# Low words of the weights and the pooled sums of a batch's q and k on VectorE instead of GpSimd

## The chip, the cores and the metric

One core of one Trainium2 chip runs the kernel. The metric is the time of one execution in microseconds, as the device measures it; less is better. The engines are named as in the profile: PE (TensorE, its matmuls), PEld (its weight loads), DVE (VectorE), ACT (ScalarE), POOL (GpSimd) and SP (SyncE), whose queue issues the DMAs. Each engine works through its own queue in order.

## What is computed

A batch of 8, 8 heads, 576 positions, 64 values per head; 512 is the width of the model and 2048 that of the hidden layer.

```python
q_d, k_d, v_d = (t.reshape(B, H, S // 4, 4, D).mean(axis=3) for t in (q, k, v))
out_up = np.repeat(softmax_attention(q_d, k_d, v_d), 4, axis=2)      # pooled attention
out_local = attention within |i - j| < 4                             # local attention
x = (out_up + out_local) as [B, S, H * D]
xn = (x - mean(x)) / sqrt(var(x) + 1e-6) * g_ln
out = x + maximum(xn @ w_ch1, 0) @ w_ch2
```

The weights w_ch1 and w_ch2 come as float64.

## The kernel before

Every part of the work is a task of a planner (class Plan): an engine, a duration that the planner assumes, a function that issues the instructions, the tasks it depends on, a due time, and buffers that it takes and gives back. `order()` puts all tasks into one list by these assumed times, task by task the one that can start first and, among those within 0.5 us, the one due first. The instructions are issued in that order, so it is also the order of each engine's queue. The planner's costs are simple lines (for VectorE 0.06 + n / 950 us for n elements per partition, for GpSimd 0.13 + 0.0022 n); they know of no effect of one engine on another. For a load it assumes 2.5 us to land (`LAT`) behind its issue, and counts its bytes at 260 GB/s. A task with `alt` may go to a second engine, whichever suits the planner's clock.

**The weights.** Sixteen blocks f of the hidden layer have a piece of w_ch1 and of w_ch2 each, 32 pieces of 128x512 float64 numbers. Each is split into a high and a low word of TensorE's 32-bit format fp32r. `weights` makes the tasks: SP loads the raw words (lines 347 and 352); ACT takes the upper half (line 359, two instructions); DVE shifts it (line 367) and puts in bits of the lower half (line 370, two instructions on 128x256); ACT makes the high word by a cast (line 378); the low word is a subtraction (line 383), which the planner gives to DVE, or to POOL where that is free sooner (with 0.3 us added). In the profile the intermediate is cva, the words are hi and lo.

**Pooled attention.** For the first batch the sums of four positions of q and k are made from the transposed windows of local attention. For every other batch and half of the heads, `pooled_half` loads q, k and v in two halves each into one of two staging buffers (raw2q is q of the second batch's first half of heads, raw3q of its second half; line 700) and adds up four positions by two instructions: 72x512 in place (line 713) and 72x256 (line 714). These are on POOL; the condition `by_dve` at line 716 holds for no task that there is, since the first batch loads v alone here. The staging buffer is given back when both are through. Transposes on PE (line 739), copies on ACT (lines 748 and 752), scores, their maximum (lines 770 and 771, DVE), exponentials and the product with v follow.

**The hidden layer.** 18 chunks c of 256 rows go through 8 pairs p of blocks. `up` (line 996) multiplies three combinations of words into PSUM, `relu` (line 1003, ACT) makes the high word hh, `rest` (line 1007, DVE) the low word hl, `down` (line 1019) adds three combinations into the accumulators. The weights are made once and stay in SBUF, so only the first chunks, between about 56 and 190 us, run while the weights are being prepared; local and pooled attention of the second batch are prepared in the same time.

Of the kernel before, what the change touches and what calls it, by code (L numbers as in the profile page):

```python
# [9 lines left out]
F32 = mybir.dt.float32  # L10
# [12 lines left out]
class Plan:  # L23
# [14 lines left out]
    def add(self, eng, dur, fn, deps=(), due=0.0, take=(), give=(), lag=None, ahead=1e9, alt=None, kb=0):  # L38

        opts = {eng: (dur, fn, 0.0)}  # L40
        if alt is not None:
            opts[alt[0]] = alt[1:]
        t = SimpleNamespace(
            n=len(self.tasks), opts=opts, dur=dur, deps=[d for d in deps if d is not None],
            due=due, take=take, give=give, lag=lag, ahead=ahead, open=0.0, waits=0, eng=None, fn=None, kb=kb,
        )
        self.tasks.append(t)
        return t
# [91 lines left out]
def attention_then_ffn(  # L140
# [10 lines left out]
    nc = tc.nc  # L151
# [37 lines left out]
    def unit(shape, name, dtype=F32, kind="u"):  # L189
        kind = kind if kind in SEP else "u"  # L190
        return work.tile(shape, dtype, tag=kind, bufs=SEP.get(kind, NU), name=name)
# [107 lines left out]
    def pooled_at(b, pr):  # L299
        if b == 0:  # L300
            return norm_at(0) - B0G - B0G_GAP * (3 - pr)
        return g_base + b * CHUNK * S / T - (NPAIR - 1 - pr) * (CHUNK * S / T / NPAIR if b > 1 else G1)
# [16 lines left out]
    U, A, STG = (("u", 1),), (("a", 1),), (("stg", 1),)  # L319
    DMA, LAT, W_AHEAD, W_LAG = 0.5, 2.5, 40, 1.5  # L320

    def act(n, sbuf=False):
        return (0.155 if sbuf else 0.14) + n / 1430.0

    def dve(n):
        return 0.06 + n / 950.0

    def pool(n):
        return 0.13 + 0.0022 * n
# [7 lines left out]
    def weights(which, f):  # L337
        key = (which, f)
        name = f"{which}_{f}"
        due = W0 + W_GAP * (f // 2) + 0.5 * (which - 1) + 1.0 * (f % 2)  # L340

        def load():
            x = box[key] = SimpleNamespace()
            x.raw = [unit([P, 512], f"s{name}_{i}", I32) for i in range(2)]
            for i in range(2):
                if which == 1:
                    nc.sync.dma_start(
                        x.raw[i].rearrange("p (c e) -> p c e", c=KC // 2),
                        w1[256 * i : 256 * (i + 1), f * 2 * P : (f + 1) * 2 * P].rearrange("(c p) e -> p c e", p=P),
                    )  # L350
                else:
                    nc.sync.dma_start(x.raw[i], w2[f * P : (f + 1) * P, 512 * i : 512 * (i + 1)])

        def high_word():

            x = box[key]
            x.a = unit([P, 512], f"cva{name}", I32)
            for i in range(2):
                nc.scalar.activation(
                    x.a[:, 256 * i : 256 * (i + 1)].bitcast(F32),  # L360
                    x.raw[i].rearrange("p (n two) -> p n two", two=2)[:, :, 1].bitcast(F32),
                    AF.Prelu, scale=REBIAS, alpha=-(2.0**32),
                )

        def low_word():
            x = box[key]
            nc.vector.tensor_single_scalar(out=x.a, in_=x.a, scalar=3, op=ALU.logical_shift_left)
            for i in range(2):
                a = x.a[:, 256 * i : 256 * (i + 1)]
                nc.vector.scalar_tensor_tensor(  # L370
                    out=a, in0=x.raw[i].rearrange("p (n two) -> p n two", two=2)[:, :, 0], scalar=29, in1=a,
                    op0=ALU.logical_shift_right, op1=ALU.bitwise_or,
                )

        def high():
            x = box[key]
            x.hi = unit([P, 512], f"hi{name}", F32R)
            nc.scalar.copy(x.hi, x.a.bitcast(F32))

        def low(eng):  # L380
            x = box[key]
            lo = unit([P, 512], f"lo{name}", F32R)
            eng.tensor_sub(lo, x.a.bitcast(F32), x.hi.bitcast(F32))
            weight[key] = (x.hi, lo)

        add = plan.add
        t = add("SP", 1.3, load, (), due, take=(("u", 3),), lag=LAT + W_LAG, kb=512, ahead=W_AHEAD)
        t = add("ACT", 2 * act(256, True), high_word, (t,), due)
        t = add("DVE", 0.45 + 2 * dve(256), low_word, (t,), due, give=(("u", 2),))
        t = add("ACT", act(512, True), high, (t,), due, take=U)  # L390
        return add("DVE", dve(512), lambda: low(nc.vector), (t,), due, take=U, give=U,
                   alt=("POOL", pool(512), lambda: low(nc.gpsimd), 0.3))

# [280 lines left out]
    def pooled(b):  # L676
        due0 = pooled_at(b, 0)
        add = plan.add
        for hg in range(2):
            pooled_half(b, hg)  # L680

    def pooled_half(b, hg):
        add = plan.add
        i = 2 * b + hg
        x = SimpleNamespace(m={})
        vd = vds[hg]
        ready = {}
        own = b < NPB
        if own:
            ready["q"], ready["k"] = gsum_done[b, "q"], gsum_done[b, "k"]  # L690
        for nm, src in (("v", v),) if own else (("q", q), ("k", k), ("v", v)):
            for half in range(2):
                key = (nm, half)
                due = pooled_at(b, 2 * hg) - (8.0 if nm == "v" else 14.0)

                def load(src=src, key=key):
                    half = key[1]
                    raw = work.tile([P, 1024], F32, tag="stg", bufs=NSTG, name=f"raw{i}{key[0]}{half}")
                    raw = raw[:GH].rearrange("p (h e) -> p h e", h=4)
                    nc.sync.dma_start(  # L700
                        raw,
                        src[b, 4 * hg : 4 * hg + 4, half * S // 2 : (half + 1) * S // 2, :]
                        .rearrange("h (g r) d -> g h (r d)", r=FACTOR),
                    )
                    x.m[key] = raw

                def pool4(key=key, eng=nc.gpsimd):
                    nm, half = key
                    raw = x.m[key]
                    if half == 0 and nm != "v":  # L710
                        setattr(x, nm, unit([GH, 2, 4, D], f"{nm}d{i}"))
                    dst = vd if nm == "v" else getattr(x, nm)
                    eng.tensor_add(raw[:, :, : 2 * D], raw[:, :, : 2 * D], raw[:, :, 2 * D :])
                    eng.tensor_add(dst[:, half, :, :D], raw[:, :, :D], raw[:, :, D : 2 * D])

                by_dve = b == 0 and nm == "k"
                t = add("SP", 0.45, load, (), due - 4.0, take=STG, lag=LAT, kb=288, ahead=AHEAD)
                t = add(
                    "DVE" if by_dve else "POOL", dve(512) + dve(256) if by_dve else 2.1,
                    (lambda key=key: pool4(key, nc.vector)) if by_dve else pool4, [t, lastg.vd[hg] if nm == "v" else None] + ready.get(nm, []),  # L720
                    due, take=U if half == 0 and nm != "v" else (), give=STG,
                )
                ready.setdefault(nm, []).append(t)
        for pr in range(2):
            pooled_pair(b, hg, pr, x, ready)
# [345 lines left out]
    for f in range(DFF // P):  # L1071
        for which in (1, 2):
            wdone[which, f] = weights(which, f)
# [42 lines left out]
```

## Time and profile before

| | us |
|---|---|
| median of 3 runs | 1068.34 (1067.77 to 1068.43) |
| the profiled execution | 1069.49 |
| its span, first to last instruction | 1067.7 |

| engine | busy us | share of the span |
|---|---|---|
| PE | 1043.4 | 98% |
| DVE | 509.0 | 48% |
| ACT | 317.7 | 30% |
| POOL | 266.5 | 25% |

TensorE's mean granted clock is 0.990 of full speed. The profile is of one execution on the chip. Busy times are those of the engines' instructions; register, branch, semaphore and DMA-issuing instructions are not counted. Instructions of one engine overlap a little at their ends, so that two in a row take less than twice one.

### The profile page before, as it was taken

Reading aid. Unit: us, or ns where it says so; the run is one execution under the profiler, and the core shown is the slowest. Engines: PE = TensorE matmul, PEld = TensorE weight load, DVE = VectorE, ACT = ScalarE, POOL = GpSimd, SP = SyncE. Lnnn points to the kernel's source line nnn. Section 1 sums busy time; section 2 is a strip of 40 time slices with the busy share of each in tenths; the row PEclk is TensorE's granted clock in tenths of the full one; section 3 lists DMA queues with packets and bytes.
Section 4 is the critical chain, followed back from the end, with each engine's and each line's share of the span. In section 5 each row is a group of like instructions: output and inputs, shape, how many; then the busy total and the mean of one; then the engine's idle time right before and its main releaser. Section 6 shows DMA issues by size and latency. Waiting matters only on the chain.

```text
span 1067.7 us, 24014 instructions
## 1 busy us (share of the span) xinstructions
PE 1043.4 (98%) x9318; PEld 937.9 (88%) x9318; DVE 509.0 (48%) x1304; ACT 317.7 (30%) x872; POOL 266.5 (25%) x285
## 2 busy tenths in 40 slices
PE   9997898999999999999999999999999999999998
PEld 8886898989899898989898989898888998898997
DVE  7699864544443445345444444445333453533211
ACT  5674642323222323132222221223212232212110
POOL 4234455143114321221303340142311400100000
PEclk9998999999999999999999999999999999999999
DMA  7889464365434363353443544243533243301000
GB/s 153 212 253 266 116 149 111 87 125 120 86 92 92 75 125 77 74 106 84 97 100 85 116 77 112 54 109 72 122 72 100 60 87 73 74 20 33 6 21 20
DMA packets 291058, 104.38 MB, mean 98 GB/s; under 512 B 239704, under 2 KB 277848, under 8 KB 290944
## 3 DMA queue, kind: packets, MB, share of 16 engines
q1 hardware_dynamic: 290944, 102.84, 41.9%
q8 instruction: 74, 1.21, 0.5%
q14 instruction: 40, 0.33, 0.1%
HBM read 82.58 MB, written 11.80 MB: 88 GB/s over the span
## 4 chain that ended last, share of the span: by engine, by line
PE 74%; SPq 1%; DMA 1%; DVE 1%; issue 0%; ACT 0%; POOL 0%; POOLq 0%; DVEq 0%
PE h L996 32%; PE acc L1019 31%; PE gv L802 2%; PE lv L595 2%; PE ls L539 2%; PE gs L766 2%; PE lt L574 1%; PE px L923 1%; PE gt L785 1%; SPq L419 1%; SPq L662 1%; DMA kr<-in_k_dram 1%; PE gq L739 0%; DMA x<-xl 0%; DVE x L1027 0%
## 5 line engine op out<-in xcount | busy, mean ns | idle before, releaser
L1019 PE MATMUL acc<-hi,hl 128*128 128x512 f32 x576 | 238.1, 413 | 6.3 <-DVE hl L1007 4.6
L1007 DVE SCALAR_TENSOR_TENSOR hl<-h,hh 128x512 fp32r<-128x512 f32 x144 | 99.1, 688 | 282.5 <-ACT hh L1003 266.9
L1019 PE MATMUL acc<-lo,hh 128*128 128x512 f32 x576 | 227.8, 395 | 0.0
L1019 PE MATMUL acc<-hi,hh 128*128 128x512 f32 x576 | 226.3, 393 | 0.0
L1003 ACT ACTIVATE hh<-h 128x512 fp32r<-128x512 f32 x144 | 86.2, 598 | 437.4 <-PE h L996 412.0
L996 PE MATMUL h<-xh,lo 128*128 128x256 f32 x1152 | 194.9, 292 | 0.5 <-ACT agt L795 0.4
L996 PE MATMUL h<-xh,hi 128*128 128x256 f32 x1152 | 186.8, 285 | 0.0
L996 PE MATMUL h<-xlo,hi 128*128 128x256 f32 x1152 | 186.5, 285 | 0.0
L996 PEld LDWEIGHTS h<-xh,lo 128*128 128x128 f32 x1152 | 170.2, 191 | 18.0 <-ACT agt L795 0.8
L996 PEld LDWEIGHTS h<-xlo,hi 128*128 128x128 f32 x1152 | 160.5, 193 | 0.0
L996 PEld LDWEIGHTS h<-xh,hi 128*128 128x128 f32 x1152 | 160.4, 193 | 0.0
L1019 PEld LDWEIGHTS acc<-hi,hh 128*128 128x128 f32 x576 | 108.8, 189 | 25.2
L896 POOL TENSOR_TENSOR x<-x,up 128x512 f32<-128x512 f32 x32 | 41.2, 1288 | 357.8 <-DMA x<-xl 230.0
L1019 PEld LDWEIGHTS acc<-hi,hl 128*128 128x128 f32 x576 | 109.8, 191 | 23.3 <-DVE hl L1007 7.3
L1019 PEld LDWEIGHTS acc<-lo,hh 128*128 128x128 f32 x576 | 110.0, 191 | 12.6
L930 ACT ACTIVATE xh<-px,gain 128x128 fp32r<-128x128 f32 x144 | 44.5, 368 | 66.1 <-PE px L923 46.5
L940 DVE SCALAR_TENSOR_TENSOR xlo<-px,gain,xh 128x128 fp32r<-128x128 f32 x144 | 42.9, 343 | 28.5 <-ACT xh L930 26.4
L545 DVE TENSOR_TENSOR ls<-ls,mask 128x256 f32<-128x256 f32 x66 | 26.8, 423 | 33.5 <-PE ls L539 33.5
L802 PEld LDWEIGHTS gv<-vd,agt 72*72 72x72 f32 x512 | 37.1, 145 | 3.1 <-POOL mv L910 1.8
L802 PE MATMUL gv<-vd,agt 72*72 72x65 f32 x512 | 37.9, 228 | 1.6 <-POOL mv L910 1.6
L910 POOL TENSOR_TENSOR mv<-mv,neg_half 128x1 f32<-128x1 f32 x36 | 19.8, 549 | 77.8 <-DVE mv L907 67.0
L779 ACT ACTIVATE ag<-gs,gmx 96x144 f32<-96x144 f32 x96 | 28.9, 374 | 33.1 <-DVE gmx L771 31.2
(199 smaller groups left out, 1149.7 us busy)
## 6 DMA issues: line engine op xcount, KB each, us to landing
s<-in_moe_w_ch_dram SPq DMA_DIRECT2D x64, 256.0 KB
out_dram<-x SPq DMA_DIRECT2D x36, 256.0 KB
vwin<-in_v_dram SPq DMA_DIRECT2D x66, 128.0 KB
qr<-in_q_dram SPq DMA_DIRECT2D x264, 32.0 KB
kr<-in_k_dram SPq DMA_DIRECT2D x264, 32.0 KB
up<-ud SPq DMA_DIRECT2D x28, 256.0 KB
x<-xl SPq DMA_DIRECT2D x92, 48.0 KB
ud<-od SPq DMA_DIRECT2D x32, 72.0 KB
```

The source lines that it names most:

```text
L539: nc.tensor.matmul(x.ps[par][64 * h2 : 64 * h2 + 64, pr], lhsT=x.qt[hs, 2 * pr + h2], rhs=x.kt[hs, 2 * pr + h2], start=True, stop=True,)
L545: nc.vector.tensor_add(x.ps[n], x.ps[n], mask.unsqueeze(1).broadcast_to([P, NPAIR, 64]))
L595: nc.tensor.matmul(x.pv[n][hs, pr], lhsT=x.at[js, pr, hs], rhs=vwin[js, m, pr] if by_pe else vwin[js, pr // 2, 2 * (pr % 2) + m], start=Tr ...
L779: nc.scalar.activation(y.a[:, c], y.ps[:, c], AF.Exp, scale=POOLED_SCALE, bias=y.mx[:, c : c + 1])
L802: nc.tensor.matmul(y.pv[:, qh, h2], lhsT=y.at[kh][:, h2, qh * GH : (qh + 1) * GH], rhs=vd[:, kh, 2 * pr + h2], start=kh == 0, stop=kh == 1,)
L896: nc.gpsimd.tensor_add(xt[n], xt[n], x.up)
L930: nc.scalar.activation(xh[c][i][:, k, j * P : (j + 1) * P], pxt[n][:, kc], AF.Copy, scale=gain[:, kc : kc + 1])
L940: nc.vector.scalar_tensor_tensor(out=xlo[c][i][:, k, ts], in0=pxt[n][:, kc], scalar=gain[:, kc : kc + 1], in1=xh[c][i][:, k, ts].bitcast(F ...
L996: nc.tensor.matmul(ph[c, p][:, fi], lhsT=wt[:, kc], rhs=xx[kc // 2][:, kc % 2], start=n == 0, stop=n == 3 * KC - 1)
L1003: nc.scalar.activation(hh[c, p], ph[c, p], AF.Relu)
L1007: nc.vector.scalar_tensor_tensor(out=hl[c, p].rearrange("p c t -> p (c t)"), in0=ph[c, p].rearrange("p c t -> p (c t)"), scalar=0.0, in1=h ...
L1019: nc.tensor.matmul(acc[c][j], lhsT=lt[:, fi, ts], rhs=rt, start=p == 0 and fi == 0 and n == 0, stop=p == NPR - 1 and fi == 1 and n == 2,)
```

## The change

The low word of a weight has DVE as its only engine. The sums of q and k of the second batch (b = 1) go from POOL to DVE, eight tasks of two instructions; those of v, and of the later batches, stay on POOL. Of the first batch nothing changes here, as it has only v. The planner's order follows from the new tasks.

```diff
-        def low(eng):
+        def low():
             x = box[key]
             lo = unit([P, 512], f"lo{name}", F32R)
-            eng.tensor_sub(lo, x.a.bitcast(F32), x.hi.bitcast(F32))
+            nc.vector.tensor_sub(lo, x.a.bitcast(F32), x.hi.bitcast(F32))
             weight[key] = (x.hi, lo)
...
-        return add("DVE", dve(512), lambda: low(nc.vector), (t,), due, take=U, give=U,
-                   alt=("POOL", pool(512), lambda: low(nc.gpsimd), 0.3))
+        return add("DVE", dve(512), low, (t,), due, take=U, give=U)
...
-                by_dve = b == 0 and nm == "k"
+                by_dve = b <= 1 and nm != "v"
```

## Rows read from the trace of the kernel before

**Rows 1.** The page, busy us, share of the span and instructions of each engine.
```profile
PE 1043.4 (98%) x9318; PEld 937.9 (88%) x9318; DVE 509.0 (48%) x1304; ACT 317.7 (30%) x872; POOL 266.5 (25%) x285
```

**Rows 2.** Busy time by stretch: length, then engines, granted clock, DMA share, GB/s.
```profile
56.00:79.00 23.00, 21.33 (x207) 19.60 (x207) 21.14 (x49) 16.53 (x46) 7.56 (x7) 1.00 0.87 243
79.00:96.60 17.60, 11.60 (x93) 9.01 (x91) 17.32 (x31) 9.69 (x28) 8.63 (x7) 0.99 1.00 301
96.60:106.40 9.80, 9.10 (x61) 8.14 (x62) 9.56 (x22) 4.24 (x11) 4.92 (x4) 0.50 0.83 222
...
121.00:131.00 10.00, 7.28 (x41) 6.29 (x39) 8.87 (x15) 4.78 (x14) 4.11 (x4) 0.83 0.43 74
...
190.00:1068.00 878.00, 870.51 (x7707) 782.82 (x7706) 369.79 (x967) 218.59 (x602) 186.01 (x191) 1.00 0.37 80
```
The engines stand in the order PE, PEld, DVE, ACT, POOL.

**Rows 3.** PE in order of time: start, length; idle before and releaser in brackets.
```profile
81.42 0.50 PE L1019 MATMUL acc<-hi,hl 128*128 128x512 f32 x1 [1.70 <-ACT hi L378]
...
88.62 0.50 PE L1019 MATMUL acc<-hi,hl 128*128 128x512 f32 x1 [1.66 <-DVE hl L1007]
...
96.66 1.24 PE L595 MATMUL lv<-vwin,at 64*64 64x65 f32 x32 [2.70 <-ACT at L581]
...
126.42 0.50 PE L1019 MATMUL acc<-hi,hl 128*128 128x512 f32 x1 [2.32 <-DVE hl L1007]
```

**Rows 4.** DVE by line, 64 to 116 us: count, busy us, mean ns, idle before.
```profile
L370 DVE SCALAR_TENSOR_TENSOR cva<-s,cva 128x256 int32<-128x256 int32 x38 | 23.6, 660 | 0.7
L367 DVE TENSOR_SCALAR cva<-cva 128x512 int32<-128x512 int32 x19 | 10.7, 562 | 0.0
L383 DVE TENSOR_TENSOR lo<-cva,hi 128x512 fp32r<-128x512 f32 x10 | 8.0, 797 | 1.5 <-ACT hi L378 1.5
...
L771 DVE TENSOR_SCALAR gmx<-gmx 96x3 f32<-96x3 f32 x1 | 1.1, 1142 | 0.0
```

**Rows 5.** Single lines, whole trace: ns least/median/most, first and last start.
```profile
L370 DVE SCALAR_TENSOR_TENSOR cva<-s,cva x64: 411/424/1501, 40.4 to 154.6; 128x256 int32<-128x256 int32 x64
...
L367 DVE TENSOR_SCALAR cva<-cva x32: 408/417/1528, 39.9 to 153.4; 128x512 int32<-128x512 int32 x32
...
L383 DVE TENSOR_TENSOR lo<-cva,hi x19: 676/684/1780, 65.1 to 178.7; 128x512 fp32r<-128x512 f32 x19
L383 POOL TENSOR_TENSOR lo<-cva,hi x13: 1269/1305/1620, 43.4 to 115.3; 128x512 fp32r<-128x512 f32 x13
...
L771 DVE TENSOR_SCALAR gmx<-gmx x32: 165/166/1249, 24.4 to 889.0; 96x3 f32<-96x3 f32 x32
```

**Rows 6.** DVE, then POOL, in order of time, 73 to 78 us.
```profile
73.65 1.77 DVE L370 SCALAR_TENSOR_TENSOR cva<-s,cva 128x256 int32<-128x256 int32 x2
...
75.79 2.27 DVE L370 SCALAR_TENSOR_TENSOR cva<-s,cva 128x256 int32<-128x256 int32 x2
...
73.51 1.30 POOL L383 TENSOR_TENSOR lo<-cva,hi 128x512 fp32r<-128x512 f32 x1 [3.42 <-ACT hi L378]
75.53 1.38 POOL L713 TENSOR_TENSOR raw2q<-raw2q 72x512 f32<-72x512 f32 x1 [0.72 <-DMA raw2q<-in_q_dram]
76.98 0.81 POOL L714 TENSOR_TENSOR qd<-raw2q 72x256 f32<-72x256 f32 x1
```

**Rows 7.** POOL by line, 64 to 116 us.
```profile
L383 POOL TENSOR_TENSOR lo<-cva,hi 128x512 fp32r<-128x512 f32 x11 | 14.9, 1359 | 33.1 <-ACT hi L378 32.0 <-DMA x<-xl 1.0
```

**Rows 8.** DVE in order of time, two instructions back to back.
```profile
126.28 1.28 DVE L383 TENSOR_TENSOR lo<-cva,hi 128x512 fp32r<-128x512 f32 x2
...
201.15 0.75 DVE L545 TENSOR_TENSOR ls<-ls,mask 128x256 f32<-128x256 f32 x2
```

**Rows 9.** SP's issues of raw loads, and POOL's start behind one.
```profile
67.59 0.39 SPq L700 DMA_DIRECT2D raw2q<-in_q_dram  x1
...
119.04 0.31 SPq L700 DMA_DIRECT2D raw3q<-in_q_dram  x1
...
122.54 1.47 POOL L713 TENSOR_TENSOR raw3q<-raw3q 72x512 f32<-72x512 f32 x1 [1.22 <-DMA raw3q<-in_q_dram]
```

## The prediction

> **What bounds the kernel now.** I read the page's busy line first. TensorE (PE) is busy 98% of the span, VectorE (DVE) 48%, GpSimd (POOL) 25% [rows 1]. That share is an average over stages, so the next view is the busy time by stretch [rows 2]. From 190 us to the end PE idles only 7.5 of 878 us: there the time is PE's own work, and DVE at 42% has room for anything. The stretch from 56 to 131 us is another regime. DVE is busy 21.1 of 23.0, then 17.3 of 17.6 and 9.6 of 9.8, and in 121 to 131 still 8.9 of 10 us, and PE is the one that pauses: 6.0 us in 79 to 96.6, 0.7 in 96.6 to 106.4, 2.7 in 121 to 131. TensorE's granted clock is 0.50 in 96.6 to 106.4, the lower of its two levels (1.2 GHz), after a stretch in which PE worked 11.6 of 17.6 us; that costs half of 9.8 us, 4.9 us of PE's work. In 121 to 131 the clock is 0.83, about 1.7 us more. Together 6.0 + 0.7 + 4.9 + 2.7 + 1.7 = 16 us of the span are lost there, and this is what a change of DVE's work can win or make larger. After 190 us nothing can make it up, because PE is full: what is won or lost before passes to the end.
>
> The waits behind these pauses are in PE's order of time [rows 3]. The matmuls of line 1019 wait for a weight's high word (1.70 us at 81.4) and for the low word of the hidden layer on DVE (1.66 at 88.6, 2.32 at 126.4); one matmul group at 96.7 waits 2.70 for a copy on ScalarE (ACT), which stood in ACT's queue behind a cast of a weight that DVE had not finished. All of these go back to DVE's queue.
>
> **Why DVE is full there.** By line, in 64 to 116 us [rows 4], DVE spends 23.6 us on 38 instructions of line 370 (660 ns each), 10.7 on 19 of line 367 (562 ns), 8.0 on 10 low words of line 383 (797 ns). The medians of the same instructions over the whole trace are 424, 417 and 684 ns, with maxima of 1501, 1528 and 1780 [rows 5]. So some of them are stretched. The two engines' order of time, side by side, shows when [rows 6]: the pair of line 370 from 73.65 takes 1.77 us while POOL's low word runs from 73.51 to 74.81, and the pair from 75.79 takes 2.27 while POOL adds up raw2q from 75.53 to 77.79. An undisturbed pair would be at most twice the median, 0.85. The first pair ends 0.6 us after POOL's instruction, the second 0.3 after POOL's last: DVE does this work when GpSimd is through.
>
> The Trainium skill, "SBUF — State Buffer", section "Who interferes with whom", says the same as a rule: a Vector instruction with two inputs in SBUF, or one in a two-port mode, contends with a GpSimd instruction that reads SBUF, and whichever issues second waits for the whole of the other. The trace agrees (1.77 us for a pair against 0.85). By the same page the loss could fall on GpSimd instead when it issues second; the rows show DVE paying more.
>
> **The change, part by part.**
>
> 1. *What GpSimd no longer does.* In 64 to 116 us these are 11 low words, 14.9 us [rows 7], and the four sums of raw2q and raw2k, 1.38 + 0.81 us the first of them [rows 6]. The view lists nothing else on POOL there, so every stretched DVE instruction in this stretch is stretched by work that the change takes away. The stretch comes to 38 x (660 - 424) = 9.0 us for line 370, 19 x (562 - 417) = 2.8 for line 367, 10 x (797 - 684) = 1.1 for line 383, and 1142 - 166 = 1.0 for line 771 [rows 4, 5]: 13.8 us, less rounding.
>
> 2. *What DVE does instead.* Two low words back to back take 1.28 us, 0.68 of it the first, so one takes 0.60 us of the queue [rows 8]. Two 128x256 additions take 0.75, so one takes 0.33. A pooled sum is a 72x512 and a 72x256 addition, both from SBUF; no row of before shows one on DVE. The nearest rows are these, 0.60 + 0.33 = 0.93 us; bounds are 0.7 (if the shorter rows of 72 partitions have less overhead) and 1.1 (684 and 420 ns without overlap). I take 0.93. In 64 to 116: 11 x 0.60 + 4 x 0.93 = 10.3 us. The balance is 13.8 - 10.3 = 3.5 us in DVE's favour.
>
> 3. *Outside that stretch.* Of 13 low words on POOL [rows 5] two ran before 64 us. I give them no stretch, so that they only cost. The first, at 43.4, falls among gaps of DVE; the second adds 0.6 us to a full queue. The four sums of raw3q and raw3k begin at 122.5 [rows 9]: 4 x 0.93 = 3.7 us on DVE, less what they stretch now, which by the ratio of part 2 (13.8 gone for 10.3 added) is more than that. I take nothing for them; the bounds are 0 and 3.7 us, and that only if all four come ahead of the wait at 126.4. The sums of v stay on POOL and go on stretching what they meet.
>
> 4. *What passes to PE.* 3.5 - 0.6 = 2.9 us less in DVE's queue ahead of the waits in [rows 3]. I take all of it as PE time, because PE's pauses there (6.7 us in 79 to 106.4) are longer than that, and DVE has no idle time in between into which it could vanish. Bounds: 1.2 us if only the work ahead of the first two waits counts (they come when half of the savings is made), 3.5 without the early low word.
>
> 5. *The clock.* It stands at 0.50 for 9.8 us behind PE's idle stretch. With 2.9 of 6.0 us of idling gone, PE would be busy 14.5 of 17.6 us there. No row says whether the clock then still falls. Bounds: it falls as before (0), or not at all (4.9 us gained); below nothing, another pause that comes late could make it fall where it didn't, at the 1.7 us that 121 to 131 shows. I take 0, by the stretch 121 to 131, where a pause of 2.7 us in 10 was followed by 0.83.
>
> 6. *Order and queues.* The planner puts instructions in order by its own costs, in which a GpSimd and a VectorE instruction never touch each other. With fifteen microseconds more on DVE (13 low words and 8 sums) it will interleave differently, on PE too. A sum now stands in DVE's queue: it waits there for its load, and behind it stand shifts for the next weights, low words, and line 1007, for which PE waits. The staging buffer comes free when DVE is through, and SP's queue, in order, holds the next raw load and weight loads behind it. I cost this at nothing in the forecast, because POOL found its data nearly there: it waited 0.72 us for raw2q at 75.5 [rows 6], the longest such wait in 64 to 116; if that cover is gone, the price is the third rival's.
>
> The sum: 1069.49 us for the profiled execution, less 2.9, is 1066.6. That execution lies 1.15 us above the median of the runs, 1068.34; with the same step the median of the changed kernel is 1065.4.
>
> **The rivals.**
>
> *The clock stays up.* If PE's pauses shrink enough, the 4.9 us of 96.6 to 106.4 and part of the 1.7 come back: 1065.4 - 4.9 = 1060.5, and with the 2.7 us pause gone too some 1057. For it: the drop stands right behind the worst idling. Against it: PE would still be idle 3 us there. Chance 0.17.
>
> *Nothing to measure.* What DVE saves comes behind the work that PE waits for, or PE, in its new order, spends it on waits that are not DVE's. Gain 0 to 2: 1067.5. Chance 0.23.
>
> *DVE stands before the raw loads* (the slower end). A load issued at 67.59 was waited for until 75.53, 7.9 us, with the DMA engines at 87 to 100% [rows 2, 6, 9]; one issued at 119.04, in a quieter stretch, until 122.54, 3.5 us [rows 9]. The planner allows a load some 4 us (0.45 to issue, 1.1 for its bytes at its rate, 2.5 to land). Where DVE is in step with the plan, it would stand up to 7.9 - 4 = 3.9 us at each of four sums, with the hidden layer's low words and the next weights behind it. The mean of nothing and 3.9 is 2.0; four of them are 8 us, less 2.9 is 5.1 slower: 1073.4. It decides from 0.7 us a sum on (2.9 / 4). Against it: DVE runs behind, being full, so that data tends to be there. Chance 0.23.
>
> *DVE is simply fuller.* If the stretched rows had another cause and stayed, DVE would carry 10.3 us more in a stretch where PE waits for it: 1068.3 + 10.3 = 1078.6. Against it stand [rows 6]. Chance 0.04. The Trainium skill, "Perfetto Trace Analysis", section "Optimizing Scalar/DVE Operations", points this way: with a full DVE, offloading some work, even to GpSimd, may make sense. It adds that between these two it might not help, because they share a port.
>
> **How the numbers follow.** The forecast, 1065.4, has 0.33 (1062 to 1066.2). With the clock's case faster has 0.50, nothing to measure 0.23, slower 0.27; the bound is 0.2%, 2.1 us, about what a measurement of this kernel can tell from no change. The range reaches from 1057 (the clock's best) to 1074 (the loads' price); beyond it lie the fuller DVE and the tails of the two cases, some 0.15.
>
> **What would show it.** In the profile after: POOL idle from 64 us to the first v sum; line 370 near 424 ns and line 367 near 0.42 where POOL is quiet; 32 low words on DVE at 0.68; a sum at 0.6 to 0.7 and 0.35 to 0.42 us; PE's idle time between 79 and 106 down from 6.7 to about 4. It is wrong if line 713 on DVE shows waits for its load of over 0.7 us each, if line 370 stays long with POOL idle, or if PE's waits move to another place at the same sum.

## The result, and the profile after

The changed kernel takes 1053.44 us in the median of four runs (1050.42 to 1057.74), the kernel before 1068.38 beside it: a ratio of 0.9862 (95% interval 0.9826 to 0.9897), 15 us faster. In two further comparisons, each on one chip, it stood at 0.9840 and 0.9848, and in a third, with a neutral edit, at 0.9854; that is 15 to 17 us. The forecast was 1065.4 with a range of 1057 to 1074; the sign was right, the size was five times too small.

The kernel before varies with the chip: its medians were 1064.6 to 1068.4. So kernels are compared here by their ratio to the kernel before, run beside them on the same chip, with its 95% interval; 0.001 is 1.07 us. The changed kernel's text is one line shorter from line 391 on, so that line 1007 of before is 1006, and 1019 is 1018.

The page's busy line after, which answers [rows 1]:

```profile
PE 1036.6 (99%) x9318; PEld 930.8 (88%) x9318; DVE 507.9 (48%) x1331; ACT 317.8 (30%) x880; POOL 231.4 (22%) x256
```

The span fell from 1067.7 to 1052.0 us. PE's busy time fell by 6.8 us with the same count of matmuls, as the mean granted clock rose from 0.990 to 0.998, and its idle time by 8.9 (24.3 to 15.4). Where, the same stretches as in [rows 2] show (PE, PEld, DVE, ACT, POOL busy; granted clock, DMA share, GB/s), and then 56 to 131 us as a whole, before and after:

```profile
56.00:79.00 23.00, 22.67 (x216) 20.45 (x216) 21.68 (x58) 18.89 (x55) 0.00 (x0) 1.00 0.92 254
79.00:96.60 17.60, 16.83 (x133) 14.80 (x132) 16.91 (x42) 13.18 (x35) 0.00 (x0) 1.00 0.98 299
96.60:106.40 9.80, 9.80 (x70) 9.06 (x69) 9.56 (x23) 6.27 (x17) 0.00 (x0) 1.00 0.67 160
...
121.00:131.00 10.00, 9.23 (x62) 8.15 (x61) 9.11 (x19) 2.66 (x8) 1.78 (x2) 1.00 0.69 159
...
190.00:1052.00 862.00, 853.48 (x7533) 767.28 (x7531) 357.52 (x936) 211.15 (x580) 183.03 (x188) 1.00 0.37 81
```
```profile
56.00:131.00 75.00, 63.91 (x496) 56.23 (x495) 70.15 (x132) 44.90 (x120) 33.36 (x27) 0.91 0.78 216
```
```profile
56.00:131.00 75.00, 72.75 (x586) 64.84 (x586) 71.56 (x167) 50.03 (x137) 6.66 (x6) 1.00 0.84 229
```

PE is busy 16.8 of 17.6 us where it was 11.6, and the clock of 96.6 to 106.4 is 1.00 where it was 0.50. From 56 to 131 us PE idles 2.2 us where it idled 11.1; from 190 us on it idles 8.5 us, about as much as before (7.5). VectorE, though, is as full as it was: 71.56 us of the 75 from 56 to 131, against 70.15. PE's pauses went without VectorE getting any freer.

The rows that answer [rows 4, 7, 8]: VectorE by line from 64 to 116 us, and the whole trace's line 383 and one pair of sums in order of time.

```profile
L370 DVE SCALAR_TENSOR_TENSOR cva<-s,cva 128x256 int32<-128x256 int32 x40 | 16.7, 459 | 0.7
L383 DVE TENSOR_TENSOR lo<-cva,hi 128x512 fp32r<-128x512 f32 x20 | 14.1, 710 | 0.0
L367 DVE TENSOR_SCALAR cva<-cva 128x512 int32<-128x512 int32 x21 | 9.9, 471 | 0.3 <-issue 0.3
...
L383 DVE TENSOR_TENSOR lo<-cva,hi x32: 676/682/1224, 55.1 to 166.2; 128x512 fp32r<-128x512 f32 x32
...
84.21 0.68 DVE L712 TENSOR_TENSOR raw2q<-raw2q 72x512 f32<-72x512 f32 x1
84.92 0.42 DVE L713 TENSOR_TENSOR qd<-raw2q 72x256 f32<-72x256 f32 x1
85.27 0.68 DVE L712 TENSOR_TENSOR raw2k<-raw2k 72x512 f32<-72x512 f32 x1
```

Line 370 takes 459 ns where it took 660, line 367 471 where it took 562. A pooled sum has the lengths that were forecast, and takes 85.27 - 84.21 = 1.06 us of the queue (0.93 was taken, 1.1 was the bound; here the second addition begins 0.03 us behind the end of the first instead of overlapping with it). What is still stretched lies at 108.9 to 113.9, where POOL adds up raw2v. POOL and VectorE there, in order of time:

```profile
108.30 1.85 POOL L712 TENSOR_TENSOR raw2v<-raw2v 72x512 f32<-72x512 f32 x1 [55.48 <-DMA s<-in_moe_w_ch_dram]
...
108.92 1.52 DVE L367 TENSOR_SCALAR cva<-cva 128x512 int32<-128x512 int32 x1
110.48 2.26 DVE L370 SCALAR_TENSOR_TENSOR cva<-s,cva 128x256 int32<-128x256 int32 x2
112.67 1.22 DVE L383 TENSOR_TENSOR lo<-cva,hi 128x512 fp32r<-128x512 f32 x1
```

The pauses that are left on PE from 56 to 131 us are short, and one of them alone is line 1006's, that is, line 1007's of [rows 3]. Line 1007's waits before, then all that are left after (engine, line waited for, us in total, times, longest):

```profile
PE acc L1019 <- DVE hl L1007: 4.6, 3, 2.3
```
```profile
PE acc L1018 <- DVE hl L1006: 0.8, 1, 0.8
PE gq L738 <- DVE kd L713: 0.7, 1, 0.7
PE gt L784 <- ACT ag L778: 0.4, 1, 0.4
PE h L995 <- DVE lo L383: 0.2, 1, 0.2
```

### The profile page after: what moved, and what is told of

Read it like the earlier page. It is cut to its first block, busy times and chain, and to the rows that moved or that the text cites. A ratio compares the mean times of both kernels' runs of the same rounds, so it can differ in the third digit from the quotient of the medians.

```text
span 1052.0 us, 23982 instructions
## 1 busy us (share of the span) xinstructions
PE 1036.6 (99%) x9318; PEld 930.8 (88%) x9318; DVE 507.9 (48%) x1331; ACT 317.8 (30%) x880; POOL 231.4 (22%) x256
## 4 chain that ended last, share of the span: by engine, by line
PE 86%; DVE 5%; DMA 3%; SPq 2%; ACT 1%; POOL 1%; issue 1%; DVEq 0%; POOLq 0%; ACTq 0%
PE h L995 36%; PE acc L1018 34%; PE gv L801 3%; PE lv L594 2%; PE ls L538 2%; PE gs L765 2%; PE lt L573 1%; PE px L922 1%; PE gt L784 1%; SPq L418 1%; DVE cva L370 1%; DMA s<-in_moe_w_ch_dram 1%; PE ex L883 1%; DVE lo L383 1%; PE gq L738 1%
## 5 line engine op out<-in xcount | busy, mean ns | idle before, releaser
L1026 DVE SCALAR_TENSOR_TENSOR x<-acc,x 128x512 f32<-128x512 f32 x36 | 24.3, 685 | 27.7 <-PE acc L1018 27.7
```

Of the source, the lines that this page charges most:

```text
L1026: nc.vector.scalar_tensor_tensor(out=x, in0=acc[c][j], scalar=1.0 + 2.0**-23, in1=x, op0=ALU.mult, op1=ALU.add)
```

## Theories

**A**: GpSimd's instructions hold up VectorE's, and PE with it; engines decide. **B**: the change gives the planner 15 us more of VectorE's work to count, and the order that comes of it, on all queues, keeps PE fed; the order decides. **C**: the order of the kernel before is a bad draw, and nearly any other is better.

## Experiment 1: order and engines apart

The planner's list can be kept while an instruction is issued on another engine. *The order of before with the engines of after:*

```diff
-                   alt=("POOL", pool(512), lambda: low(nc.gpsimd), 0.3))
+                   alt=("POOL", pool(512), lambda: low(nc.vector), 0.3))
...
-                    (lambda key=key: pool4(key, nc.vector)) if by_dve else pool4, ...
+                    (lambda key=key: pool4(key, nc.vector)) if b == 1 and nm != "v" else pool4, ...
```

> The list of tasks is that of the kernel before, task for task: the planner still believes that 13 low words and the eight sums of the second batch's q and k are GpSimd's, but they are issued on VectorE. Theory A (GpSimd's instructions hold VectorE up, and that is all): the order doesn't matter, the stretched rows of lines 367 and 370 go, the time is that of the changed kernel, 1053 +- 3 us, and PE's idle time in 56 to 131 us falls from 11 to about 2. Theory B (the planner's new order, which counts that work as VectorE's, is what removes PE's waits): the rows of line 370 are short, but VectorE's queue is as full as before and in the old order, so PE waits as before: 1065 +- 2 us.

Measured: 0.9925 (0.9895 to 0.9956), 1057.66 us, about 8 us faster than before (5 to 11). This lies between the figures of the two theories.

*The order of after with the engines of before* (`ON_POOL` holds the 13 pieces that GpSimd had):

```diff
-            nc.vector.tensor_sub(lo, x.a.bitcast(F32), x.hi.bitcast(F32))
+            eng = nc.gpsimd if key in ON_POOL else nc.vector
+            eng.tensor_sub(lo, x.a.bitcast(F32), x.hi.bitcast(F32))
...
-                    (lambda key=key: pool4(key, nc.vector)) if by_dve else pool4, ...
+                    pool4, ...
```

> The list of tasks is that of the changed kernel, but the 13 low words that GpSimd had before and the eight sums are issued on GpSimd. Theory A: lines 367 and 370 are stretched again by some 14 us between 64 and 116 us, and the time is that of the kernel before, 1067 +- 3. Theory B: the order keeps PE fed although the rows are stretched: 1055 +- 3.

Measured: 0.9897 (0.9854 to 0.9939), 1055.17 us, about 11 us faster than before (7 to 16). This is theory B's figure. From 56 to 131 us (first the order of before on VectorE, then the order of after with GpSimd):

```profile
56.00:131.00 75.00, 67.52 (x536) 59.90 (x535) 71.12 (x170) 49.21 (x131) 5.03 (x4) 0.98 0.81 217
```
```profile
56.00:131.00 75.00, 68.23 (x555) 60.87 (x554) 68.34 (x131) 47.84 (x131) 35.69 (x29) 1.00 0.80 219
```

PE idles 7.5 and 6.8 us, where the kernel before idles 11.1 and the changed one 2.2. In the second, line 370 (371 in its text) takes 664 ns on average between 64 and 116 us, as stretched as in [rows 4]:

```profile
L371 DVE SCALAR_TENSOR_TENSOR cva<-s,cva 128x256 int32<-128x256 int32 x38 | 23.7, 664 | 0.7
```

So neither theory has it alone. Each half by itself takes off 8 to 11 us, and together they take off 15 to 17. That is less than their sum of 19, but within the intervals, so an overlap of the halves is not shown.

## Experiment 2: one part of the change alone

*Low words alone* (the sums' condition as before) and *sums alone* (the low words' tasks as before).

> The low words are VectorE's alone, the sums stay GpSimd's, and the planner knows both. Theory A: by the rows of before the low words cause some 9 of the 14 us of stretch, the sums 5, so most of the gain stays: 1058 +- 3. Theory B: the larger part of the work that the planner counts anew is the low words' (7.8 of 15 us), 1060 +- 3; with the order the result can also fall outside, as another order is another set of waits.

Measured: 0.9904 (0.9870 to 0.9937).

> The sums of the second batch's q and k are VectorE's, the low words keep GpSimd as their second engine. Theory A: only 5 us of stretch go, and VectorE takes 3.7 us on, so little is gained: 1066 +- 2. Theory B: half of the newly counted work, 1061 +- 3.

Measured: 0.9913 (0.9887 to 0.9939). Either part brings some 10 us, the sums far more than their 5 us of stretch less 3.7 us of work could. The second is not the sums alone in its effect: with their second engine left to them, 20 low words now went to GpSimd, not 13, and line 370 still takes 603 ns in the mean over the whole trace, where it took 629 before and takes 475 in the changed kernel. Most of that stretch stayed, and the time fell all the same. By these edits the order changes as well, so they don't tell the theories apart; and the two gains add up to 19 us, again above the 15 to 17 of the whole, but within the intervals.

## Experiment 3: contention by itself

The changed kernel with additions on GpSimd that nobody needs. Order and VectorE's work stay.

```diff
+            if key in ON_POOL:
+                h = x.hi[96:].bitcast(F32)
+                nc.gpsimd.tensor_add(spare, h, h)
             lo = unit([P, 512], f"lo{name}", F32R)
```

(`spare` lies in the unused partitions of a tile for pooled v.) First for 13 weights:

> The changed kernel, task for task and in its order, with 13 additions more on GpSimd that nobody needs: where GpSimd made the low word of a weight before, it adds that weight's high word (32 partitions, 512 elements) to itself into a spare place in SBUF. VectorE's work and every order stay; only GpSimd reads SBUF beside it. Theory A (GpSimd's instructions hold VectorE up and PE with it): lines 367, 370 and 383 are stretched by some 9 us between 56 and 116 us, PE's idle time there grows by 5 to 9, and the time is 1061 +- 3. Theory B (the planner's order decides): the same stretch, but the order holds: 1055 +- 2.

Measured: 0.9917 (0.9889 to 0.9945), 1057.34 us. Without the changed kernel beside it this falls between the two theories' figures (1058 to 1064 and 1053 to 1057), so the comparison was made again, beside the changed kernel and a version with one such addition for each of the 32 weights.

> The changed kernel, beside the next two on one chip: 0.985 +- 0.003 of the kernel before.

> The changed kernel's order and VectorE work, with 13 needless additions on GpSimd: as the first time, 0.991 to 0.992 (theory A: some 6 us for some 9 us of stretch). If the first comparison was the chip's doing: 0.985.

> The same with a needless addition for each of the 32 weights, 2.5 times as much of GpSimd's reading beside VectorE, order and VectorE work again as in the changed kernel. Theory A: the loss grows with it, 10 to 16 us over the changed kernel, so as slow as the kernel before or slower (0.995 to 1.001). If contention only matters at a few places: as with 13, 0.992.

| | ratio to before | median, us |
|---|---|---|
| the changed kernel | 0.9848 (0.9818 to 0.9877) | 1051.39 |
| with 13 additions | 0.9924 (0.9901 to 0.9947) | 1057.91 |
| with 32 additions | 1.0015 (0.9998 to 1.0031) | 1067.91 |

The loss grows with the dose, and with 32 additions the whole gain is gone. VectorE by line, 56 to 131 us; the changed kernel, then 13, then 32 (lines 372, 388 and 717 in the latter two are 370, 383 and 712):

```profile
L370 DVE SCALAR_TENSOR_TENSOR cva<-s,cva 128x256 int32<-128x256 int32 x51 | 21.4, 459 | 0.9
L383 DVE TENSOR_TENSOR lo<-cva,hi 128x512 fp32r<-128x512 f32 x26 | 18.1, 703 | 0.0
```
```profile
L372 DVE SCALAR_TENSOR_TENSOR cva<-s,cva 128x256 int32<-128x256 int32 x48 | 23.4, 529 | 0.8
L388 DVE TENSOR_TENSOR lo<-cva,hi 128x512 fp32r<-128x512 f32 x23 | 16.4, 719 | 0.0
...
L717 DVE TENSOR_TENSOR raw2k<-raw2k 72x512 f32<-72x512 f32 x2 | 2.2, 1106 | 0.0
```
```profile
L372 DVE SCALAR_TENSOR_TENSOR cva<-s,cva 128x256 int32<-128x256 int32 x46 | 27.0, 627 | 0.8
L388 DVE TENSOR_TENSOR lo<-cva,hi 128x512 fp32r<-128x512 f32 x22 | 18.0, 821 | 0.0
L717 DVE TENSOR_TENSOR raw2k<-raw2k 72x512 f32<-72x512 f32 x2 | 2.2, 1101 | 0.0
```

With 32 the stretch is 46 x (627 - 459) = 7.7 us for line 370, 22 x (821 - 703) = 2.6 for the low words, 2 x (1101 - 680) = 0.8 for raw2k's sums, and about 1 in smaller groups: 12 us, for a loss of 16.5. With 13 the same working gives 3.4 + 0.4 + 0.9 and 0.7 in a smaller group, 5.4 us, for 6.5. Over the whole trace VectorE's busy time, for the same 1331 instructions, grows by 14.7 and 4.3 us. The pages' lines, the changed kernel, then 13, then 32:

```profile
PE 1036.8 (99%) x9318; PEld 932.4 (89%) x9318; DVE 509.0 (48%) x1331; ACT 318.7 (30%) x880; POOL 231.5 (22%) x256
```
```profile
PE 1038.2 (99%) x9318; PEld 933.0 (89%) x9318; DVE 513.3 (49%) x1331; ACT 317.6 (30%) x880; POOL 246.3 (23%) x269
```
```profile
PE 1040.2 (98%) x9318; PEld 933.6 (88%) x9318; DVE 523.7 (49%) x1331; ACT 318.3 (30%) x880; POOL 269.2 (25%) x288
```

So in a fixed order a microsecond of stretch costs 1.1 to 1.5 us of the kernel's time by these medians. With 32 additions the intervals of the ratios leave 1.0 to 1.8; with 13 they are too wide to say more than that there is a loss. This is what theory A says, shown at two doses: contention by itself costs time.

The largest of PE's waits, and the one that grows most, is for line 1006 (1011 with the additions). From 56 to 200 us, the changed kernel, then 32 additions:

```profile
PE gv L801 <- ACT agt L794: 2.3, 1, 2.3
...
PE acc L1018 <- DVE hl L1006: 0.5, 1, 0.5
```
```profile
PE acc L1023 <- DVE hl L1011: 5.9, 3, 3.6
PE gv L806 <- ACT agt L799: 4.2, 1, 4.2
...
PE gv L806 <- POOL vd L718: 1.0, 1, 1.0
```

The last line is another cost of the additions: the sums of v stand behind them in GpSimd's queue. It is 1.0 us of the 16.5, and with 13 additions there is no such wait.

## Experiment 4: is it the draw, is it the count?

*Neutral edits of the planner*, on the engines of before: a pooled sum on GpSimd priced at 2.2 us instead of 2.1, and, in the other, `self.lags = (80, 0.32, 0.6)` instead of 0.3.

> The kernel before, on its engines (13 low words and all sums on GpSimd), with one number of the planner's changed that has nothing to do with VectorE: it takes a pooled sum on GpSimd for 2.2 us instead of 2.1. 429 of 769 VectorE tasks and 31 of 906 PE tasks stand at another place in their queue. Theory C (the order of before was a bad draw, and nearly any other is some 10 us better): 1056 +- 3. Theory B (an order is better when it counts VectorE's work fully): this one doesn't, so 1066 +- 3. Theory A: contention as before, 1066 +- 3.

> Another neutral change of the planner's: it allows 0.32 us instead of 0.30 between an instruction and the one that waits for it, up to 80 us. 14 low words are on GpSimd, the sums too; 671 of 769 VectorE tasks stand elsewhere. Theory C: 1056 +- 3. Theories A and B: 1066 +- 3.

Measured: 1.0003 (0.9978 to 1.0029) and 1.0010 (0.9982 to 1.0038). Theory C does not hold for these two: they are other orders, with hundreds of VectorE tasks elsewhere, and as slow as the kernel before. The control below is a third, and faster. The second edit on the changed kernel:

> The changed kernel with the neutral change of the planner's that moved the kernel before by nothing (0.32 us instead of 0.30 between an instruction and the next). If its gain hangs on one lucky order it goes: 1058 or more. If it comes of the engines and of the count (A and B): 1051 +- 3.

Measured: 0.9854 (0.9817 to 0.9892). So the gain outlasts this one small change of order.

*The count.* In the control the 13 low words are tied to GpSimd, so that the planner has no choice; in the test it also counts 0.43 us more for lines 367 and 370 of each weight, the stretch that it doesn't know of.

```diff
-        t = add("DVE", 0.45 + 2 * dve(256), low_word, ...
+        t = add("DVE", 0.88 + 2 * dve(256), low_word, ...
...
+        if key in ON_POOL:
+            return add("POOL", pool(512), lambda: low(nc.gpsimd), (t,), due, take=U, give=U)
+        return add("DVE", dve(512), lambda: low(nc.vector), (t,), due, take=U, give=U)
```

> A control for the next run: the kernel before with its 13 low words tied to GpSimd and the others to VectorE, so that the planner has no choice; the sums are GpSimd's. Prices as before. Theory B (an order is good when the planner counts all the time that VectorE will need) and theory A: 1065 +- 3, as before.

> The control with one price changed: the planner takes lines 367 and 370 of a weight for 0.43 us longer (13.8 us of stretch over 32 weights). No instruction changes its engine, GpSimd stretches VectorE as before. Theory B: the order now counts what VectorE really needs, PE's idle time in 56 to 131 us falls from 11 to 4 to 7, and the time is 1056 +- 3. Theory A: the contention is all there, 1065 +- 3.

Measured: 0.9944 (0.9909 to 0.9979) for the control and 0.9884 (0.9851 to 0.9918) with the price, 1061.82 and 1054.88 us. The control alone is already 5 to 6 us better than before (2 to 10), which neither theory had. The price brings another 6 to 7 (1 to 12), with every instruction on its old engine. Both have VectorE as full, and stretched (line 370 takes 642 ns in the control and 713 in the test); PE from 56 to 131 us, control and test:

```profile
56.00:131.00 75.00, 66.32 (x556) 58.95 (x552) 71.29 (x143) 49.46 (x135) 34.80 (x28) 0.98 0.78 215
```
```profile
56.00:131.00 75.00, 67.72 (x570) 59.06 (x570) 73.04 (x142) 48.66 (x132) 34.78 (x28) 1.00 0.80 216
```

PE's idle time there falls from 8.7 to 7.3 us, just above the 4 to 7 that theory B gave for it, and the clock rises from 0.98 to 1.00. Now the other way, the changed kernel with 0.02 in the place of 0.45, so that the planner counts 13.8 us too little:

> The changed kernel on its engines, with the planner taking lines 367 and 370 of a weight for 0.43 us less (13.8 us over 32 weights less than VectorE needs). No stretch is added. Theory B: the order undercounts VectorE as that of the kernel before does, hidden-layer low words stand behind weights that aren't needed yet, 1058 +- 3. Theory A: no contention, 1051 +- 3 as the changed kernel on this chip.

Measured: 0.9868 (0.9845 to 0.9890), 1052.64 us. Theory B said 1058, and falls as a general rule: without the low words and sums on GpSimd, an undercount costs nothing that can be told from the changed kernel's 0.9840 to 0.9862. Counting the stretch helped in the one pair where there was stretch; what else in an order makes it good was not found.

Taken together, six orders with the low words and sums shared with GpSimd as before (13 or 14 low words) lie between 0.988 and 1.001 of the kernel before. Four orders with them all on VectorE lie between 0.984 and 0.9925. The two ranges overlap: the engines move the range, and the order makes a difference of some 10 us within it.

## Experiment 5: further on the same way

The second batch's sums of v (`by_dve = b == 1`), then the third batch's q and k as well (`b == 1 or b == 2 and nm != "v"`), then all of both batches (`1 <= b <= 2`).

> The changed kernel with the second batch's sums of v on VectorE as well. In the changed kernel these stretch VectorE's instructions at 108 to 114 and 129 to 134 us by some 5 us; on VectorE they cost 4 x 0.93 = 3.7 us. Theory A: a gain of 1 to 3 us, 1051 +- 2. Theory B: one more order, 1053 +- 3.

> The changed kernel with the second batch's sums of v, and the third batch's of q and k, on VectorE too. Behind 131 us VectorE is half idle and PE waits little, so the third batch's should matter less than the second's v: by theory A 1049 to 1052 where the changed kernel has 1053.

> The changed kernel itself beside these runs, for their comparison on one chip: a ratio of 0.986 +- 0.003 to the kernel before.

> All pooled sums of the second and the third batch on VectorE, those of v too. The third batch's v sums run behind 150 us, where VectorE is half idle: by A 1046 +- 3, as with the third batch's q and k alone.

| on VectorE | ratio to before | median, us |
|---|---|---|
| the changed kernel, beside the third row | 0.9840 (0.9800 to 0.9881) | 1048.97 |
| the second batch's v too | 0.9828 (0.9782 to 0.9874) | 1048.62 |
| and the third batch's q and k | 0.9806 (0.9770 to 0.9841) | 1045.96 |
| all sums of both batches | 0.9787 (0.9760 to 0.9815) | 1045.05 |

Each step has the better estimate, some 6 us from the first row to the last, about as theory A has it; the intervals of neighbours overlap, and each step is a new order too, so that the runs don't say which of the two did it. The third batch's q and k were expected to bring less than the second's v; they don't (2.3 and 1.3 us, within the noise). The last is the fastest version that was run, ahead of both kernels. In it POOL is all but idle from 56 to 131 us, and its row there is

```profile
56.00:131.00 75.00, 71.63 (x610) 64.13 (x610) 66.68 (x163) 50.51 (x138) 0.04 (x1) 1.00 0.84 231
```

VectorE has more instructions there than the kernel before had (163 for 132) and is busy 66.7 us, not 70.2.

## Why the prediction was wrong

**What held.** The mechanism of parts 1 and 2: the long rows were GpSimd's doing, they are short in the profile after, the low words cost 0.68 us and the sums 0.68 and 0.42. Experiment 3 shows the stretch as a cause by itself. None of the signs that the prediction named for being wrong appeared, and PE's idle time between 79 and 106 us fell further than it said, from 6.7 to 0.8 us instead of 4. The fuller VectorE of the fourth rival did not come about. The wait for raw loads, the third rival, did not either: the longest on a sum is 0.65 us, and no sum of raw2q or raw2k waited:

```profile
123.42 0.69 DVE L712 TENSOR_TENSOR raw3q<-raw3q 72x512 f32<-72x512 f32 x1 [0.65 <-DMA raw3q<-in_q_dram]
```

**Steps 1 and 2, the balance: somewhat too large.** By the rows from 64 to 116 us, 38 x (660 - 459) + 19 x (562 - 471) + 10 x (797 - 710) + 1.0 = 11.2 us of stretch went, not 13.8, since the sums of raw2v moved from 116.6 to 108.3 us and stretch what they meet there. A sum took 1.06 us, not 0.93. Over the whole trace VectorE took on 17.6 us (13 low words at 0.68 us, 8 sums at 1.10) and its busy time fell by 1.1 (509.0 to 507.9), where the forecast took 2.9 off its queue.

**Step 4, what passes to PE: right in kind, too small, and in the wrong measure.** It passed VectorE's balance of 2.9 us to PE one to one. By experiment 1 the engines alone are worth 8 us in the order of before (5 to 11), and 0.9897 less 0.985, about 5 us, in the order of after (0 to 10). The term should have been some 5 to 8 us. VectorE's busy time differs in these two pairs by only 2.4 us (509.0 before, 506.6) and 0.3 us (508.2, and 507.9 after). The pages' lines of the order of before with the engines of after, then of the order of after with the engines of before:

```profile
PE 1038.5 (98%) x9318; PEld 933.4 (88%) x9318; DVE 506.6 (48%) x1333; ACT 316.6 (30%) x872; POOL 231.3 (22%) x256
```
```profile
PE 1036.1 (98%) x9318; PEld 930.7 (88%) x9318; DVE 508.2 (48%) x1302; ACT 317.4 (30%) x880; POOL 266.4 (25%) x285
```

So what PE gains can't be read from the sum of VectorE's busy time, and 1.1 to 1.5 us for a microsecond of stretch doesn't make 5 to 8 of such a balance either. VectorE stayed full, yet PE's waits for line 1007 fell from 4.6 to 0.8 us. In the order of after the engines also count in a second way, apart from the stretch: GpSimd's results come later. The largest of PE's waits from 56 to 200 us, with that order and the sums on GpSimd, is

```profile
PE gq L740 <- POOL kd L715: 3.3, 2, 1.9
```

where the changed kernel waits 0.7 us for the same sums on VectorE. That is 2.6 us more, of the some 5 us between these two kernels. Whether GpSimd is only slower at this work (1.3 us for a low word, against 0.68) or is held up itself, no run tells. In the kernel before the wait for these sums is 0.3 us.

**Step 6, order and queues: the step that failed.** It named the new order and costed it at nothing, with a price only for harm. With the old engines and all their stretch, the order of after alone takes off 11 us (7 to 16), as much as the engines do or more. The forecast had no row for an order that didn't exist yet, and should have given this term a width of some 10 us, not zero. The neutral edits of experiment 4 show that an order can also change nothing; no order that was run was slower than that of before by more than the noise.

**Step 5, the clock: the wrong end of its bounds.** 0 was taken of 0 to 4.9. The stretch at 0.50 is gone altogether, and PE's busy time over the span is 6.8 us less. It was argued from 121 to 131 us, where one pause of 2.7 us was followed by 0.83; after the change no pause between 56 and 131 us is longer than 0.8 us, and the clock is 1.00 in every stretch there. The rival of the clock that stays up, with a chance of 0.17, came true in its mechanism (1060.5, at best 1057). Its best case gave back the clock and the 2.7 us pause, but only 2.9 of the 6.7 us of pauses between 79 and 106 us, and there the range ended. Nearly all of them went. What the prediction itself counted as lost in this regime, 16 us, is about what the change won. (It is nearer 15: the clock's 4.9 and 1.7 us take in PE's idle time, which is counted beside them; for the 9.10 and 7.28 us in which PE was busy they are 4.6 and 1.2.)

**Left open.** Which feature of the new order keeps PE fed. It isn't the count of VectorE's time by itself (experiment 4), nor a lucky draw that the one small edit tried would undo. ACT's waits for line 370 are a candidate that was only seen, not tried: from 56 to 131 us its casts wait 17.0 us in the kernel before and 7.2 after, but 16.1 in the underpriced kernel, which is nearly as fast, and 16.1 in the one with the stretch priced. From the kernel before and the kernel after:

```profile
ACT hi L378 <- DVE cva L370: 17.0, 13, 3.2
```
```profile
ACT hi L378 <- DVE cva L370: 7.2, 7, 3.3
```

## What to carry to other kernels

Before work is moved to GpSimd to relieve a full VectorE, lay the two engines' rows side by side in time: what VectorE's other instructions are stretched by can be as much as what it gives away (here it took 17.6 us of work back, and its busy time fell by 1.1), and whoever waits in order behind a stretched instruction pays for it, here at about one for one or somewhat more. Where a planner makes the order, an edit that changes its counts is a new order: give it a term of its own, as wide as neutral edits and engine swaps in a fixed list show (0.988 to 1.001 here, on the same engines). A feeding engine that stays full says little about the fed one; look at which instruction the pauses end on, and at what the clock did after them.

## What the runs showed that was not expected

The edits of experiments 1 and 2 each gave 8 to 11 us (0.9897 to 0.9925), and the whole change 15 to 17. Each half of the change alone gave half of the gain or more; whether the halves overlap or add up lies within the intervals.

Needless additions of 32 partitions and 512 elements (1.16 to 1.20 us each on GpSimd in the mean) slowed the kernel by 0.5 us each, though nothing uses what they make. They read and write SBUF; the runs don't tell which of the two costs. Of the 15.7 us between the two profiled spans, 6.8 are PE's busy time, with the same count of matmuls and a mean granted clock of 0.998 where it was 0.990; the other 8.9 are its idle time.
